# The last addition of eight decoded weight pieces, moved from VectorE to GpSimd

## The chip, the cores and the metric

The kernel runs on one core of a Trainium2 chip. The metric is the device time of one execution, in microseconds, as the median of several runs. The engines are TensorE (PE, with its weight loads as PEld), VectorE (DVE), ScalarE (ACT), GpSimd (POOL) and SyncE (SP), which issues all the transfers here.

## The reference, cut to what matters

Linear attention is followed by a gated feed-forward layer. The feed-forward weights arrive as 64-bit floats.

```python
def phi(x):                                   # per head: 576 x 64 -> 576 x 256
    proj = x @ w_phi
    proj = proj - np.max(np.abs(proj), axis=-1, keepdims=True)
    return np.concatenate([np.exp(proj), np.exp(-proj)], axis=-1)
q_p, k_p = phi(q), phi(k)                     # 8 batches x 8 heads
kv, z = k_p.T @ v, k_p.sum(axis=rows)
attn = (q_p @ kv) / (q_p @ z + 1e-6)
x = attn, heads side by side                  # 4608 x 512
xn = x / sqrt(mean(x * x) + 1e-6) * rms_g
g, val = xn @ w_gate, xn @ w_val              # 512 x 1536 each
out = (silu(g) * val) @ w_out                 # 1536 x 512
```

## The kernel before, in words

**Attention.** The 64 heads are worked off as 32 pairs. A loop of 35 rounds (L524) runs as a pipeline over the pairs. In round i, `front(i)` transposes and projects K and Q of pair i. On PE that is L305 and L318 to L320, on ACT the casts of L60, on DVE the maximum L322 and the subtraction L325 that give `yk` and `yq`. `mid(i-1)` takes the exponentials of pair i-1 and accumulates K^T V: ACT makes `eq` and `qh` (L388, L389), and GpSimd subtracts them into `ql`, eight pieces of 128x256 (L393) and one small one (L395) for each pair. `back(i-2)` multiplies Q's features with K^T V (PE L427) and reads `qh` and `ql`; its K^T V operands are `kv0h`, `kv0l` and `kv1h`, `kv1l` by turns from pair to pair. `last(i-3)` divides (DVE L463, L464) and stores rows of `xs`.

**Decoding.** A 64-bit weight is turned into a 32-bit one in `_decode`, one piece of 128x384 at a time. There are 32 such pieces. ACT scales the high and the low words (L48, L49), DVE does three bit operations (L50 to L52), GpSimd multiplies in two halves of 128x192 (L54), and an addition (L55) finishes the piece. Pieces 0 to 7, four of `w_gate` and four of `w_val`, are the weights of the *fill*: `fill_w` scales each by the norm's weight and splits it on ACT (L241) and DVE (L242) into `fg` or `fv`. The other 24 are only stored to DRAM (L247). The rounds take 0.8 piece each at first and 1.1 from round 10 on (L534).

**Fill.** From round 9 on, blocks of finished attention rows are multiplied with `fg` and `fv` (PE L495) between the attention's own products.

**Order.** The Python loops merge the steps of a round by position (`_merge`, L64). The order in which each engine gets its instructions is not that of the source: the whole program goes through the framework's scheduler (`schedule_with_timeline_sim=True`, L1471), which puts them in order by a timeline of its own when the kernel is built. `late()` (L176) adds one edge: what is traced inside it is issued behind the last instruction that ACT, DVE and GpSimd each had at that place. A decoded piece lies inside it. Behind the attention a second planner (`Flow`) writes out the order by hand, each engine's instruction chained to the one before (line 575 in the profile).

The line of the change passes the adding engine to `_decode` as `add_eng`; before, the condition there is never true for the 32 pieces of this kernel, so all additions are DVE's.

Of the kernel before, what the change touches and what calls it, by code (L numbers as in the profile page):

```python
# [30 lines left out]
def _fetch(nc, pool, src, n):  # L31
    if src.dtype == F32:
        w = pool.tile([128, n], F32, name="wa", bufs=2)
        nc.sync.dma_start(out=w, in_=src)
        return w
    raw = pool.tile([128, n, 2], I32, name="raw", bufs=2)
    nc.sync.dma_start(out=raw.rearrange("p n t -> p (n t)"), in_=src.bitcast(I32))
    return raw


def _decode(nc, pool, raw, n, add_eng=None):
    if raw.dtype == F32:
        return raw
    low, high = raw[:, :, 0], raw[:, :, 1]
    p = pool.tile([128, n], I32, name="wp", bufs=2)
    a = pool.tile([128, n], F32, name="wa", bufs=2)
    u, lf = a.bitcast(I32), low.bitcast(F32)
    nc.scalar.mul(a, high.bitcast(F32), REBASE)  # L48
    nc.scalar.mul(lf, low.bitcast(U32), 2.0 ** -52)  # L49
    nc.vector.tensor_scalar(p, u, 3, None, ALU.logical_shift_left)  # L50
    nc.vector.scalar_tensor_tensor(p, u, -0x80000000, p, ALU.bitwise_and, ALU.bitwise_or)
    nc.vector.tensor_scalar(u, p, -0x00800000, None, ALU.bitwise_and)  # L52
    for h in (slice(0, n // 2), slice(n // 2, n)):
        nc.gpsimd.tensor_tensor(a[:, h], lf[:, h], a[:, h], ALU.mult)  # L54
    (add_eng or nc.vector).tensor_tensor(a, p.bitcast(F32), a, ALU.add)  # L55
    return a
# [26 lines left out]
def kernel(ctx: ExitStack, tc: tile.TileContext, q, k, v, w_phi,  # L83
                         w_gate, w_val, w_out, rms_g, out):
    nc = tc.nc
# [3 lines left out]
    NC, NJ = DM // 128, DF // 128  # L89
# [85 lines left out]
    @contextmanager  # L175
    def late():  # L176

        ins = nc.cur_bb.bb.instructions
        n = len(ins)
        with ExitStack() as es:  # L180
            for eng in LATE:
                for i in reversed(ins[-300:]):
                    if i.engine == eng and i.name not in waiting:
                        es.enter_context(tc.issue_after(i))
                        break
            yield
        waiting.update(i.name for i in nc.cur_bb.bb.instructions[n:])
# [9 lines left out]
    dec = a_ctx.enter_context(tc.tile_pool(name="a_dec", bufs=1))  # L197
# [61 lines left out]
    def decode_pieces(jobs, dec):  # L259
        raws = {}  # L260

        def piece(i):
            if i == 0:
                raws[0] = _fetch(nc, dec, *jobs[0][:2])
            raw = raws.pop(i)
            if i + 1 < len(jobs):
                raws[i + 1] = _fetch(nc, dec, *jobs[i + 1][:2])
            with late():
                jobs[i][2](_decode(nc, dec, raw, jobs[i][1], nc.gpsimd if i >= 2 * NC + 24 else nc.vector))
        return [lambda i=i: piece(i) for i in range(len(jobs))]  # L270

    st = {}
# [397 lines left out]
    nc = Engines()  # L670
# [627 lines left out]
    nc = tc.nc  # L1298
# [177 lines left out]
```

## Time and profile before

| what | value |
|---|---|
| median of 3 runs | 1224.36 us (1223.18 to 1227.45) |
| the profiled execution | 1228.98 us |
| its span on the core | 1227.2 us |
| TensorE busy | 1207.3 us (98%) |
| VectorE, ScalarE, GpSimd busy | 1012.9, 810.3, 620.2 us |
| mean granted TensorE clock | 0.997 |

The span runs from the first to the last instruction of the profiled execution. A share of busy time is a mean over all stages, so the stretches have to be read one by one. Times in the trace count from the start of the span.

### The profile page before, as it was taken

The numbers are of one execution on the slowest core, as the hardware profiler recorded it, in microseconds if no ns is written. First come the engines' busy times: TensorE is split into PE (matmuls) and PEld (weight loads), VectorE is DVE, ScalarE is ACT, GpSimd is POOL, SyncE is SP. The second block draws the span as 40 slices with busy tenths as digits, with TensorE's granted clock in tenths as the row PEclk, the third lists the DMA queues.
The fourth block names the chain that finished last, engine by engine and source line by source line (L and its number), as shares of the span: only waits on it lengthen the run. The fifth ranks groups of instructions, "written<-read, shape, count | busy, mean of one in ns | idle before, by whom it ended". The sixth has DMA issues, their size and how long they took to land.

```text
span 1227.2 us, 28324 instructions
## 1 busy us (share of the span) xinstructions
PE 1207.3 (98%) x10347; PEld 1198.7 (98%) x10347; DVE 1012.9 (83%) x1581; ACT 810.3 (66%) x1867; POOL 620.2 (51%) x681
## 2 busy tenths in 40 slices
PE   8999999999999999999999999999999999999998
PEld 7898999999999999999999999999999999999998
DVE  6889988778788887897996888799777799888884
ACT  6788887778778787667666667667656454444441
POOL 3656664556556666774876777677676200000000
PEclk9999999999999999999999999999999999999999
DMA  5446575657565653986465667755545645544421
GB/s 154 129 122 167 144 207 169 184 158 194 153 176 150 174 160 100 291 267 201 127 206 182 208 198 223 235 175 192 173 154 171 242 142 177 163 139 138 138 95 44
DMA packets 204123, 209.29 MB, mean 171 GB/s; under 512 B 70928, under 2 KB 174224, under 8 KB 201808
## 3 DMA queue, kind: packets, MB, share of 16 engines
q1 hardware_dynamic: 203984, 207.48, 56.1%
q8 instruction: 82, 1.34, 0.5%
q14 instruction: 57, 0.47, 0.1%
HBM read 136.87 MB, written 70.40 MB: 169 GB/s over the span
## 4 chain that ended last, share of the span: by engine, by line
PE 86%; DVE 5%; DMA 4%; ACT 2%; issue 1%; POOL 1%; SPq 0%; DVEq 0%; ACTq 0%; POOLq 0%
PE B L575 12%; PE E L575 10%; PE A L575 9%; PE acc L361 8%; PE gz L1398 6%; PE gy L1398 6%; PE gd L1398 6%; PE fp L495 6%; PE sm L427 5%; PE fp L1398 3%; PE pp L318 3%; PE fp L427 3%; PE pp L320 3%; PE pp L319 2%; PE sm L377 2%; PE sm L305 2%
## 5 line engine op out<-in xcount | busy, mean ns | idle before, releaser
L393 POOL TENSOR_TENSOR ql<-eq,qh 128x256 fp32r<-128x256 f32 x256 | 218.9, 885 | 90.5 <-issue 47.1
L575 PE MATMUL B<-xo,w 128*128 128x256 f32 x1458 | 193.6, 277 | 1.8 <-ACT h L575 1.2
L575 PEld LDWEIGHTS B<-xo,w 128*128 128x128 f32 x1458 | 178.4, 188 | 3.2 <-ACT h L575 2.0
L322 DVE TENSOR_REDUCE mx<-pp 128x4 f32<-128x512 f32 (+1 forms) x160 | 101.2, 634 | 53.8 <-PE pp L320 52.1
L575 PE MATMUL A<-xo,w 128*128 128x256 f32 x972 | 137.1, 277 | 0.0
L575 PE MATMUL E<-xo,w 128*128 128x256 f32 x972 | 137.1, 277 | 0.0
L361 PE MATMUL acc<-vm,ek 128*128 128x65 f32 x1024 | 130.4, 269 | 0.0
L361 PEld LDWEIGHTS acc<-vm,ek 128*128 128x128 f32 x1024 | 126.6, 193 | 0.0
L575 PEld LDWEIGHTS E<-xo,w 128*128 128x128 f32 x972 | 122.9, 188 | 0.2
L575 PEld LDWEIGHTS A<-xo,w 128*128 128x128 f32 x972 | 122.8, 188 | 0.3
L575 POOL TENSOR_TENSOR h<-h,c 128x256 f32<-128x256 f32 x81 | 65.8, 812 | 88.9 <-ACT h L575 77.7
L389 ACT ACTIVATE qh<-sm 128x512 fp32r<-128x512 f32 (+1 forms) x192 | 97.1, 506 | 0.0
L60 ACT CAST xo<-st 128x768 fp32r<-128x768 f32 x54 | 44.9, 838 | 70.5 <-PE gy L1398 25.6
L388 ACT ACTIVATE eq<-sm 128x512 f32<-128x512 f32 x128 | 78.3, 612 | 15.2 <-PE sm L377 14.8
L318 PE MATMUL pp<-wh,th 128*128 128x256 f32 x288 | 86.5, 302 | 1.8 <-DVE yk L325 0.7
L320 PE MATMUL pp<-wh,tl 128*128 128x256 f32 x288 | 83.3, 298 | 0.0
L319 PE MATMUL pp<-wl,th 128*128 128x256 f32 x288 | 81.5, 284 | 0.0
L575 ACT ACTIVATE h<-A 128x256 f32<-128x256 f32 x81 | 31.2, 385 | 73.9 <-PE A L575 56.2
L1398 PE MATMUL gy<-w,xo 128*128 128x256 f32 x648 | 78.4, 279 | 0.2 <-ACT xo L60 0.2
L348 ACT ACTIVATE ek<-yk 128x512 f32<-128x512 f32 x128 | 75.4, 647 | 2.8 <-DVE yk L325 2.8
L1398 PE MATMUL gd<-w,xo 128*128 128x256 f32 x648 | 76.7, 276 | 0.0
L1398 PE MATMUL gz<-w,xo 128*128 128x256 f32 x648 | 76.7, 276 | 0.0
(195 smaller groups left out, 3370.3 us busy)
## 6 DMA issues: line engine op xcount, KB each, us to landing
w<-hs SPq DMA_DIRECT2D x17, 1536.0 KB
hs<-h SPq DMA_DIRECT2D x81, 256.0 KB
gvs<-fo SPq DMA_DIRECT2D x108, 128.0 KB
gvr<-gvs SPq DMA_DIRECT2D x54, 256.0 KB
x<-xs SPq DMA_DIRECT2D x18, 512.0 KB
x<-xs SPq DMA_DIRECT2D x9, 1024.0 KB
rc<-di SPq DMA_DIRECT2D x31, 288.0 KB
kt<-in_k_dram SPq DMA_DIRECT2D x32, 256.0 KB
```

The source lines that it names most:

```text
L318: nc.tensor.matmul(o, th[:, cs], wh, start=True, stop=False)
L319: nc.tensor.matmul(o, th[:, cs], wl, start=False, stop=False)
L320: nc.tensor.matmul(o, tl[:, cs], wh, start=False, stop=True)
L322: nc.vector.tensor_reduce(mx[:, 0:2 * m], pp[:, 0:2 * m], axis=AX.X, op=ALU.max, apply_absolute_value=True)
L348: nc.scalar.activation(e[h][:, sg], y["k", h], AF.Exp, scale=1.0 - 2.0 * sg)
L361: nc.tensor.matmul(acc[:, sg, h], e[h][:, sg, j], vm[:, h, j], start=False, stop=(h == 1 and j == T0 - 1))
L388: nc.scalar.activation(ei[:, sg], yi, AF.Exp, scale=1.0 - 2.0 * sg)
L389: nc.scalar.activation(hi[:, sg], yi, AF.Exp, scale=1.0 - 2.0 * sg)
L393: nc.gpsimd.tensor_tensor(lo[:, sg, cs], ei[:, sg, cs], hi[:, sg, cs].bitcast(F32), ALU.subtract)
L427: nc.tensor.matmul(o[:, 0:m], a[:, h, sg], e[:, sg, h, cs], start=(i == 0), stop=(i == 5))
L575: r = f(*a, **k)
L1398: nc.tensor.matmul(place[n], a[:, kp], w[:, o], start=(first and (kp, i) == turns[0]), stop=((kp, i) == turns[-1]), skip_group_check=True)
```

## The change

For pieces 0 to 7 the addition L55 is issued by GpSimd, right behind its two products L54 in the source. Nothing else differs: the same operands, the same tiles, the same `late()` block. Pieces 8 to 31 keep VectorE.

```diff
             with late():
-                jobs[i][2](_decode(nc, dec, raw, jobs[i][1], nc.gpsimd if i >= 2 * NC + 24 else nc.vector))
+                jobs[i][2](_decode(nc, dec, raw, jobs[i][1], nc.gpsimd if i >= 2 * NC + 24 or i < 2 * NC else nc.vector))
```

`NC` is 4. The addition itself is the last line of `_decode`:

```python
(add_eng or nc.vector).tensor_tensor(a, p.bitcast(F32), a, ALU.add)
```

## Rows read from the trace of the kernel before

**Rows 1.** The page, part 1: busy time and share of each engine.

```profile
PE 1207.3 (98%) x10347; PEld 1198.7 (98%) x10347; DVE 1012.9 (83%) x1581; ACT 810.3 (66%) x1867; POOL 620.2 (51%) x681
```

**Rows 2.** Windows: busy time (instructions) of each engine, then clock, DMA share, GB/s.

```profile
50.44:59.97 9.53, 7.91 (x46) 6.91 (x45) 6.53 (x13) 6.87 (x16) 8.04 (x10) 0.82 0.43 124
...
110.00:120.00 10.00, 10.00 (x84) 9.78 (x83) 9.87 (x17) 8.16 (x23) 4.78 (x5) 1.00 0.63 180
...
160.00:475.00 315.00, 314.50 (x2688) 313.54 (x2687) 256.47 (x454) 254.01 (x636) 182.18 (x228) 1.00 0.61 168
```

**Rows 3.** Waits of PE, 0 to 150 us: total us, times, longest.

```profile
PE sm L377 <- DVE yq L325: 2.6, 4, 1.3
...
PE fp L427 <- ACT kv1h L60: 0.7, 1, 0.7
PE pp L318 <- DVE yk L325: 0.7, 2, 0.5
PE fp L427 <- ACT kv0h L60: 0.6, 2, 0.4
PE fp L427 <- DVE kv0l L61: 0.6, 1, 0.6
```

**Rows 4.** Line 55, 0 to 150 us: duration ns min/median/max, first and last start.

```profile
L55 DVE TENSOR_TENSOR wa<-wp,wa x8: 546/850/1074, 30.3 to 139.4; 128x384 f32<-128x384 f32 x8
```

**Rows 5.** GpSimd's two-input operations of two widths, with min/median/max ns.

```profile
L393 POOL TENSOR_TENSOR ql<-eq,qh x84: 717/740/1295, 19.5 to 156.9; 128x256 fp32r<-128x256 f32 x84
...
L575 POOL TENSOR_TENSOR ri<-ri,t x27: 1283/1477/1770, 506.2 to 854.0; 128x512 f32<-128x512 f32 x27
```

**Rows 6.** Timeline of ACT, DVE, POOL: first, sixth and last of the pieces.

```profile
29.08 1.16 POOL L54 TENSOR_TENSOR wa<-raw,wa 128x192 f32<-128x192 f32 x2 [2.51 <-ACT th L60]
31.64 0.67 ACT L241 ACTIVATE fg<-wa,g 128x384 fp32r<-128x384 f32 x1
...
109.08 1.69 POOL L54 TENSOR_TENSOR wa<-raw,wa 128x192 f32<-128x192 f32 x2
...
111.39 4.01 POOL L393 TENSOR_TENSOR ql<-eq,qh 128x256 fp32r<-128x256 f32 x4 [0.62 <-POOL wa L54]
...
113.92 0.88 DVE L55 TENSOR_TENSOR wa<-wp,wa 128x384 f32<-128x384 f32 x1
...
114.83 0.62 ACT L241 ACTIVATE fv<-wa,g 128x384 fp32r<-128x384 f32 x1 [1.84 <-DVE wa L55]
...
136.84 1.17 POOL L54 TENSOR_TENSOR wa<-raw,wa 128x192 f32<-128x192 f32 x2 [0.41 <-POOL ql L393]
139.41 0.55 DVE L55 TENSOR_TENSOR wa<-wp,wa 128x384 f32<-128x384 f32 x1
...
140.47 0.63 ACT L241 ACTIVATE fv<-wa,g 128x384 fp32r<-128x384 f32 x1
```

**Rows 7.** Timeline of PE: the order of L319 and L318, and one wait.

```profile
31.69 0.28 PE L319 MATMUL pp<-wl,th 128*128 128x256 f32 x1
31.80 0.28 PE L318 MATMUL pp<-wh,th 128*128 128x256 f32 x1
...
107.78 0.63 PE L377 MATMUL sm<-ident,yq 128*128 128x128 f32 x4 [1.25 <-DVE yq L325]
```

**Rows 8.** Timeline of DVE ahead of that wait.

```profile
106.22 0.81 DVE L51 SCALAR_TENSOR_TENSOR wp<-wa,wp 128x384 int32<-128x384 int32 x1
106.95 0.68 DVE L325 TENSOR_TENSOR yq<-pp,mx 128x512 f32<-128x512 f32 x1
...
108.15 0.37 DVE L52 TENSOR_SCALAR wa<-wp 128x384 int32<-128x384 int32 x1
```

**Rows 9.** Timeline of GpSimd's `ql` of one pair, and PE's first reading of them.

```profile
52.61 5.86 POOL L393 TENSOR_TENSOR ql<-eq,qh 128x256 fp32r<-128x256 f32 x6
...
67.81 0.31 PE L427 MATMUL fp<-ql,kv1h 128*128 128x320 f32 x1
```

**Rows 10.** Timeline of PE: its first fill products with `fv`.

```profile
145.05 1.63 PE L495 MATMUL fp<-xo,fv 128*128 128x256 f32 x12
```

## The prediction, made before the result was known

> **What bounds the kernel now.** I read the page first, then windows, then TensorE's waits, then the decoded pieces one by one.
>
> TensorE is busy for 1207.3 of the span's 1227.2 us, GpSimd for half of it [rows 1]. That is a mean, so the windows come next. All eight pieces lie between 25 and 145 us. From 160 to 475 us TensorE stands for only 0.5 us in 315 [rows 2]: there neither VectorE nor GpSimd can shorten anything. What can be won or lost lies before 160 us.
>
> The waits say what ends TensorE's gaps there. Apart from the start-up the larger of them make 5.2 us, of which VectorE ends 2.6 + 0.7 + 0.6 = 3.9 us (`yq`, `yk`, `kv0l`) and ScalarE the rest; GpSimd ends none of them [rows 3]. There is one more loss: the granted clock of 50.44 to 59.97 us is 0.82 of full, so about (1 - 0.82) x 9.53 = 1.7 us of it went to the lower level, 1.2 GHz, after a run of short gaps in TensorE's work [rows 2]. The most that any relief could give back is thus 5.2 + 1.7 = 6.9 us, and a few tenths of smaller gaps.
>
> **What the change removes.** Eight additions leave VectorE: 546 to 1074 ns each, median 850, one by one 1.07 + 0.55 + 0.56 + 0.99 + 0.85 + 0.88 + 0.85 + 0.55 = 6.30 us [rows 4]; the sixth and the last of them stand in [rows 6]. The question is whether TensorE was waiting for what stood behind them. I looked behind each of the eight: no gap of TensorE begins within 2 us after one that its successors on VectorE could have ended. The largest of VectorE's gaps, 1.25 us at 107.78, shows what it is instead [rows 7]: `yq` at 106.95 runs right behind the bit operation L51, 0.81 us at 106.22 [rows 8], and that stays. Where VectorE is fullest, 9.87 of 10 us, TensorE is busy for all 10 [rows 2]. So I cost the removal at nothing. The cover is TensorE's backlog of work already released; if it were gone, a median addition would be worth 0.85 us, and all eight 6.3 us at most.
>
> **What it adds.** No row shows GpSimd adding 128x384. GpSimd's two-input operations take 717 to 1295 ns at 256 columns (median 740) and 1283 to 1770 ns at 512 (median 1477) [rows 5]. Half way between the smallest is 1.00 us, between the largest 1.53, between the medians 1.11. I take 1.05, nearer the low end because the median at 256 columns lies close to its minimum: 8 x 1.05 = 8.4 us more on GpSimd, bounds 8.0 and 12.3.
>
> What queues behind it is `ql`. The eight wide `ql` pieces of the pair around 52 us are done at 52.61 + 5.86 = 58.47, and TensorE reads the first of them at 67.81 [rows 9]: 9.3 us of slack, against 1.05 of delay. That is the busiest round for GpSimd that I found. ScalarE reuses the two `eq` buffers that `ql` reads; its waits name GpSimd nowhere in this stretch. So the added work costs nothing too; without that slack it would be 8.4 us.
>
> **What it moves.** The addition's reader is ScalarE's L241. Today the chain goes from GpSimd's products to VectorE's queue to ScalarE; with the change VectorE drops out. The distance from the end of L54 to the start of L241 is, piece by piece, 1.40, 2.23, 3.12, 3.59, 3.87, 4.06, 2.42, 2.46 us, in sum 23.15; the first, the sixth and the last can be read in [rows 6]. An addition of 1.05 us directly behind its products fits into every one of them. In the sixth the products end at 110.77 and VectorE comes to the addition only at 113.92, and ScalarE stands 1.84 us for it [rows 6]; that wait would go. It is worth nothing, since TensorE is busy for all of 110 to 120 [rows 2]. The fill is no nearer to its limit: the last piece's L241 starts at 140.47 [rows 6], TensorE's first product with `fv` at 145.05 [rows 10]. No transfer is issued differently.
>
> **The scheduler.** The order on the engines isn't the source's: TensorE runs L319 and then the next L318 before the L320 that stands between them in the source [rows 7]. The scheduler works with its own price for the moved operation, so the order of other instructions in the attention may change as well. No row prices this. The gain is bounded by the 6.9 us of gaps and clock; for the loss I take as much again, since a new order would have to double all of today's gaps. Near zero is the value I take: three quarters of the attention run at a full TensorE [rows 2], where another order has nothing to move.
>
> The undisturbed addition on VectorE takes 0.546 us [rows 4], on GpSimd 1.05 by my estimate, a ratio of 1.9; against the median of 0.85 it is 1.2. The Trainium skill, GPSIMD Engine Reference, section "When to use GPSIMD", speaks against the change: two-input elementwise work belongs on VectorE, GpSimd being about twice as slow. The lower ratio comes from VectorE's own spread: the same instruction takes 0.55 us at 139.41, after GpSimd's last operation has ended at 138.01, and 0.88 at 113.92, in the middle of GpSimd's 4.01 us of `ql` [rows 6]. The same page, section "Specifications", says that an SBUF interface is shared with VectorE instructions of two SBUF inputs, and these two rows agree. By that rule GpSimd's new 8.4 us would slow what VectorE runs beside them, by at most 0.53 us a piece (1.074 less 0.546), 4.2 in all, and VectorE would be relieved by 2.1 us instead of 6.3. That changes nothing in a sum in which the relief is worth zero.
>
> **Sum.** The profiled execution took 1228.98 us, 1.78 more than its span. Removed 0, added 0, moved 0, order 0: 1229.0 for it. It lies 4.6 us above the median of the runs shown, so the forecast is the median, 1224.4 us.
>
> **The rivals.**
>
> *VectorE's relief reaches TensorE.* The gaps that VectorE ends close, 3.9 us, and with them the stretch of lower clock, 1.7 us. 1224.4 - 5.6 = 1218.8. For it: 6.3 us of VectorE's work go, partly where VectorE is busy for 9.87 of 10 us [rows 2], and `yq` and `yk` are its work. Against: no gap lies behind an addition. It decides from 3.7 us on, two thirds of it.
>
> *ScalarE stands at L241 behind GpSimd's queue; this is the slower side.* If the scheduler puts a block of four `ql` between the products and the addition, 4 x 0.74 = 2.96 us [rows 5], the addition ends 2.96 + 1.05 = 4.0 us behind the products. Set against the eight distances above, ScalarE would be late by 2.6, 1.8, 0.9, 0.4, 0.1, 0, 1.6 and 1.6: 9.0 us of standing, with `kv0h`, `th` and the exponentials queued behind it, for which TensorE waits. If half of it reaches TensorE, 1224.4 + 4.5 = 1228.9. For it: dependent steps of a piece on VectorE have other work between them (L51 and L52 in rows 8). Against: with one or two `ql` between, 0.74 each, all but the first piece or two still fit, and the 1.84 us that ScalarE stood before cost TensorE nothing. It decides where more than 3.7 of the 9.0 us arrive.
>
> *The order shifts by luck.* Gaps come and go, with either sign, by up to about 3 us: 1221.4 to 1227.4, which can't be told from no change.
>
> That the change might do nothing is excluded: the eight pieces are in the trace on VectorE [rows 4].
>
> **How the numbers follow.** About 0.3%, 3.7 us, is what a measurement of this kernel can tell from no change. Forecast and luck within it together: 0.70. Relief reaching TensorE: 0.17. ScalarE behind GpSimd: 0.13. Faster 0.17, same 0.70, slower 0.13. The range reaches to both rivals' values, 1218.8 and 1228.9, and leaves out the halves of them that go further: 1219 to 1229. The likeliest case alone is 1221.4 to 1227.4.
>
> **What would show it.** L55 should appear as eight additions on GpSimd of 1.0 to 1.5 us, and 24 on VectorE. VectorE's busy time should fall by 2 to 6 us, GpSimd's rise by 8 to 12. TensorE's waits before 160 us should stay between 3 and 8 us, with no GpSimd among the releasers, and 160 to 475 us should stay full. I would be wrong if TensorE's waits named L241's successors or `ql`, if the stretch of lower clock vanished or came twice, or if the order of the attention changed so far that gaps appear behind 160 us.

## The result, and the profile after

The changed kernel is slower: 1233.65 us (median of 4 runs, 1233.33 to 1234.99) against 1224.24 (4 runs in the same comparison), a ratio of 1.0077 with a 95% interval of 1.0062 to 1.0092. The forecast was 1224.4, its range 1219 to 1229: the time lies above the range, and the sign was given 0.13. Here and below, ratios leave out the few slow executions (mean clock 0.95 or less: one each of e5, e10 and before), while medians in us include them.

The profiled execution of the kernel after took 1233.75 us (span 1232.0). Its engines, by part 1 of the page, against [rows 1]:

```profile
PE 1208.4 (98%) x10347; PEld 1199.2 (97%) x10347; DVE 1012.4 (82%) x1573; ACT 811.6 (66%) x1867; POOL 631.9 (51%) x689
```

The eight additions have changed engine: eight instructions fewer on VectorE, eight more on GpSimd. But VectorE is no less busy (1012.4 us against 1012.9), which is the first surprise. Line 55 of the kernel after, 0 to 150 us, its duration (min/median/max in ns) and who waited for it, against [rows 4]:

```profile
L55 POOL TENSOR_TENSOR wa<-wp,wa x8: 999/1180/1527, 32.1 to 140.6; 128x384 f32<-128x384 f32 x8
...
  ACT fv L241: 1.4, 1
  ACT fg L241: 0.4, 1
```

On GpSimd an addition takes 1.0 to 1.5 us, and ScalarE stood behind it for 1.8 us in all. So the moved work is about as forecast. The loss must be elsewhere. The windows of the kernel after, for the same stretches as [rows 2] (busy time and instructions of PE, PEld, DVE, ACT, POOL, then clock, DMA share, GB/s):

```profile
50.44:59.97 9.53, 7.33 (x44) 6.42 (x43) 8.32 (x13) 8.09 (x18) 8.55 (x11) 0.83 0.47 137
...
110.00:120.00 10.00, 10.00 (x88) 10.00 (x86) 9.72 (x18) 8.29 (x23) 7.99 (x8) 1.00 0.48 132
160.00:475.00 315.00, 313.73 (x2674) 312.05 (x2673) 256.79 (x451) 252.03 (x632) 182.50 (x224) 1.00 0.62 169
```

From 160 to 475 us TensorE now stands for 1.27 us instead of 0.50: something moved even where the attention was full. The waits of TensorE, 0 to 150 us (total us, times, longest), against [rows 3]:

```profile
PE sm L377 <- DVE yq L325: 3.2, 4, 1.4
PE pp L318 <- DVE yk L325: 1.3, 2, 0.7
PE fp L427 <- DVE kv1l L61: 1.2, 1, 1.2
PE fp L427 <- DVE kv0l L61: 1.2, 1, 1.2
PE pp L318 <- ACT th L60: 1.0, 2, 0.5
...
PE fp L427 <- ACT kv0h L60: 0.5, 2, 0.3
```

VectorE ends 6.9 us of waits here, against 3.9 before. The wait for `kv1l` is new, that for `kv0l` has doubled, those for `yq` and `yk` are 0.6 longer each in sum. Start-up aside, none names GpSimd, and the waits have grown from 5.8 to 8.6 us together. Where the new wait comes from can be seen on VectorE, in the timeline of the kernel after (start, duration):

```profile
95.68 0.69 DVE L325 TENSOR_TENSOR yq<-pp,mx 128x512 f32<-128x512 f32 x1
96.29 1.17 DVE L463 TENSOR_TENSOR nd<-nd,rc 64x576 f32<-64x576 f32 x1
97.48 1.19 DVE L464 TENSOR_TENSOR nd<-nd,rc 64x576 f32<-64x576 f32 x1
98.70 0.22 DVE L445 RECIPROCAL dr<-dr 128x9 f32<-128x9 f32 x1
98.83 0.37 DVE L61 TENSOR_TENSOR kv1l<-acc,kv1h 128x260 fp32r<-128x260 f32 x1
```

The low half of K^T V, 0.37 us of work that TensorE needs at once, now stands behind two divisions whose result is only stored. In the kernel before, the same `kv1l` ran at 93.99, ahead of the second `yq` and of the divisions. The scheduler has put it elsewhere, and not only it: in the tables that hold the two orders in e1 and e3 below, 1,417 of TensorE's 2,757 places differ, 269 of ScalarE's 812, 141 of VectorE's 608 and 172 of SyncE's 479. TensorE's two waits for such low halves, in its timeline (in brackets idle time and who ended it):

```profile
57.06 0.64 PE L427 MATMUL fp<-qh,kv0l 128*128 128x320 f32 x1 [1.22 <-DVE kv0l L61]
...
99.25 0.41 PE L427 MATMUL fp<-qh,kv1l 128*128 128x320 f32 x1 [1.22 <-DVE kv1l L61]
```

`kv0l` is another case than `kv1l`: in both kernels it stands behind the two divisions of its round. What has changed is the first division. Before, and below it after:

```profile
52.56 0.74 DVE L463 TENSOR_TENSOR nd<-nd,rc 64x576 f32<-64x576 f32 x1
...
54.67 0.37 DVE L61 TENSOR_TENSOR kv0l<-acc,kv0h 128x260 fp32r<-128x260 f32 x1
...
55.09 0.41 PE L427 MATMUL fp<-qh,kv0l 128*128 128x320 f32 x1 [0.56 <-DVE kv0l L61]
```

```profile
53.93 1.34 DVE L463 TENSOR_TENSOR nd<-nd,rc 64x576 f32<-64x576 f32 x1
...
56.64 0.37 DVE L61 TENSOR_TENSOR kv0l<-acc,kv0h 128x260 fp32r<-128x260 f32 x1
```

The division takes 0.60 us longer, TensorE's wait grows by 0.66. The moved addition is not what lengthens it: that starts only at 55.83 us, and in e3 below, where the addition is back on VectorE, the division takes 1.34 us too.

Last, the clock. Windows of the kernel after, PE alone (width, busy time, clock, DMA share, GB/s):

```profile
54.00:66.00 12.00, 10.28 (x71) 0.86 0.40 125
96.00:111.00 15.00, 13.28 (x108) 1.00 0.68 183
970.00:980.00 10.00, 8.48 (x58) 0.83 0.78 286
```

Two stretches ran in part at the lower level, 1.2 GHz: 0.14 x 12 = 1.7 us and 0.17 x 10 = 1.7 us were lost to it. The profiled execution of before also has a stretch near 55 us [rows 2] and one near 970, and its mean granted clock is 0.997 as well. At that equal clock the two executions are 1233.75 - 1228.98 = 4.8 us apart, and TensorE's idle time has grown by 2.6 us before 160 us (10.8 to 13.4) and by 0.8 from 160 to 475. The other 4.7 of the 9.5 us come from what is usual: before's other executions, in all comparisons, mostly had a mean clock of 0.999 to 1.0, after's four had 0.995 to 0.997. So by this one pair about half of the loss is there at an equal clock, and the other half is clock. The split is rough: after's execution at 0.997 took as long (1233.75) as its three at 0.995 (1233.33 to 1234.99). Whether the second follows from the first is for the experiments.

### The profile page after: what moved, and what is told of

Same layout as the page of the kernel before. It is cut to its first block, busy times and chain, and to the rows that moved or that the text cites. A ratio compares the mean times of both kernels' runs of the same rounds, so it can differ in the third digit from the quotient of the medians.

```text
span 1232.0 us, 28322 instructions
## 1 busy us (share of the span) xinstructions
PE 1208.4 (98%) x10347; PEld 1199.2 (97%) x10347; DVE 1012.4 (82%) x1573; ACT 811.6 (66%) x1867; POOL 631.9 (51%) x689
## 3 DMA queue, kind: packets, MB, share of 16 engines
q8 instruction: 82, 1.34, 0.5%
## 4 chain that ended last, share of the span: by engine, by line
PE 89%; DVE 5%; DMA 3%; ACT 1%; issue 1%; SPq 0%; POOL 0%; DVEq 0%; ACTq 0%; POOLq 0%
PE B L575 12%; PE A L575 10%; PE E L575 9%; PE acc L361 8%; PE fp L495 6%; PE gz L1398 6%; PE gy L1398 6%; PE gd L1398 6%; PE sm L427 5%; PE fp L427 3%; PE fp L1398 3%; PE pp L318 3%; PE pp L320 3%; PE pp L319 2%; PE sm L377 2%; PE sm L305 2%
## 5 line engine op out<-in xcount | busy, mean ns | idle before, releaser
L318 PE MATMUL pp<-wh,th 128*128 128x256 f32 x288 | 87.0, 304 | 2.7 <-DVE yk L325 1.3
L319 PE MATMUL pp<-wl,th 128*128 128x256 f32 x288 | 81.8, 286 | 0.0
```

What stands on the lines that cost most here:

```text
L318: nc.tensor.matmul(o, th[:, cs], wh, start=True, stop=False)
L319: nc.tensor.matmul(o, th[:, cs], wl, start=False, stop=False)
```

## The experiments

**Theories.** One: the addition's new engine costs, through its duration, its queue or its contention with VectorE. Two: the new order costs, either everywhere or in a few places. In most of the runs below the order on each engine is held by edges added in the source after tracing, one instruction behind the other; a table says which order.

**e1, the control.** The kernel before with its own order held.

```diff
+    for e, order in ORDER:                    # one list of instructions for each engine
+        last = None
+        for n in order:
+            i = traced[n]
+            if last is not None:
+                tc.add_manual_dep(i, last.name, NoSync, reason="order")
+            last = i
```

> Control: the kernel before, unchanged in its work, with the order that the scheduler had given it written out as a chain of issue-order edges for each engine over the whole attention. Both theories expect the time of before, 1224 us, within 2 us. If it differs by more, holding an order costs something itself, and the next two kernels are to be read against this one.

Measured: 1224.91 us, ratio 1.0002 (0.9994 to 1.0011). Holding an order costs nothing that can be measured.

**e2, the additions on GpSimd in before's order.** The change, with each addition right behind its products on GpSimd and everything else where before has it.

```diff
-    add_eng = nc.gpsimd if i >= 2 * NC + 24 else nc.vector
+    add_eng = nc.gpsimd if i >= 2 * NC + 24 or i < 2 * NC else nc.vector
+    ORDER = before's, the eight additions behind their products on GpSimd
```

> The eight additions on GpSimd, directly behind their two products, everything else on every engine in the order of the kernel before. Theory A (the new order of the other instructions costs the time, the moved work nothing): 1224 us, within 2 us of the control. Theory B (the moved work costs it: ScalarE's cast stands behind GpSimd, or the ql queue behind the addition): 1232 to 1235 us, as the changed kernel. Between 1227 and 1231: both have a share.

Measured: 1224.58 us, 1.0004 (0.9993 to 1.0015). Line 55 and VectorE around 94 us in this run:

```profile
L55 POOL TENSOR_TENSOR wa<-wp,wa x8: 1001/1208/1450, 31.3 to 136.8; 128x384 f32<-128x384 f32 x8
```

```profile
93.56 0.43 DVE L61 TENSOR_TENSOR kv1l<-acc,kv1h 128x260 fp32r<-128x260 f32 x1
93.90 0.68 DVE L325 TENSOR_TENSOR yq<-pp,mx 128x512 f32<-128x512 f32 x1
94.50 1.10 DVE L463 TENSOR_TENSOR nd<-nd,rc 64x576 f32<-64x576 f32 x1
```

The additions are as long as in the kernel after, nobody waits for them, and no time that can be measured is lost. The first theory falls with this run.

**e3, the additions on VectorE in after's order.** The reverse: the order without the change.

```diff
     add_eng = nc.gpsimd if i >= 2 * NC + 24 else nc.vector
+    ORDER = after's, the eight additions back at before's places on VectorE
```

> The eight additions back on VectorE, each behind the same VectorE instruction as in the kernel before, all other instructions of every engine in the order that the scheduler gave the changed kernel. Theory A: 1232 to 1235 us, as the changed kernel, though no work has moved. Theory B: 1224 us, as before, within 2 us.

Measured: 1235.73 us, 1.0095 (1.008 to 1.0109). Waits and windows of PE:

```profile
PE fp L427 <- DVE kv1l L61: 2.1, 1, 2.1
PE fp L427 <- DVE kv0l L61: 1.2, 1, 1.2
```

```profile
54.00:66.00 12.00, 10.28 (x72) 0.86 0.41 122
96.00:111.00 15.00, 12.41 (x73) 0.77 0.59 171
```

The order alone, with no addition on GpSimd, costs as much or more. With the additions back on VectorE, `kv1l` is later still, and a second stretch of lower clock follows it.

**e4, the first four pieces alone, scheduler free.**

```diff
-    nc.gpsimd if i >= 2 * NC + 24 or i < 2 * NC else nc.vector
+    nc.gpsimd if i >= 2 * NC + 24 or i < NC else nc.vector
```

> Only pieces 0 to 3 (those of w_gate) are added on GpSimd; the scheduler is free, as in the changed kernel. Theory B, cost per moved addition: half of the 9.4 us, so about 1229 us. Theory A: what the order happens to be, anywhere between 1221 and 1236 us; a time outside 1227 to 1231 speaks for A.

Measured: 1229.28 us, 1.0041 (1.0028 to 1.0053), with the same two waits of 1.2 us for low halves. The order tips with the early pieces: `kv1l` at 97 us is late although the piece beside it is not moved.

**e5, the first piece's place.** In before's order (with the additions on GpSimd) the first piece is put where after has it. There `yk` comes out late behind it.

```diff
  VectorE:  L322 mx
-           L242 fg        (first piece)
            L322 mx
+           L242 fg
  ScalarE:  L241 fg behind one more nd (L435);  GpSimd:  L55 behind two ql (L393)
```

> The order of e2 (additions on GpSimd, all else as before), except for the first piece: as in the changed kernel, two ql pieces stand between the products and the addition on GpSimd, L241 stands behind one nd copy on ScalarE, and L242 stands behind two mx on VectorE. Three engines, eight instructions. Theory A1 (the cost sits in few places on VectorE's queue): TensorE's waits for yk, yq and kv0l before 58 us grow by 2 us, and a stretch of 3.4 us at the lower clock comes back at 54 us and costs 1.7: 1227 to 1229 us. Theory A2 (the cost is spread over the hundreds of other shuffled instructions): 1224 to 1225.5 us.

Measured: 1229.49 us, 1.0032 (1.0016 to 1.0048). It costs about 3.9 us by itself, by the ratio. No waits are read from its profile.

**e6, one low half.** In the order of e2 a single instruction is moved.

```diff
  VectorE:  L325 yq
-           L61  kv1l      (94 us)
            L325 yq
            L463 nd
            L464 nd
            L445 dr
+           L61  kv1l
```

> The order of e2 with one instruction moved: VectorE's kv1l of the round around 94 us stands behind yq, the two divisions L463 and L464 and the reciprocal L445, as in the changed kernel. Theory A1: TensorE waits 1.2 us for it, with 0.5 for th beside it and at times a stretch at the lower clock (1.7 us each): 1225.5 to 1228 us. Theory A2: 1224 to 1225 us.

Measured: 1234.04 us, 1.0075 (1.0053 to 1.0098). One instruction of 0.4 us in another place costs as much as the whole change, three times the wait that it causes. TensorE's timeline and windows show how:

```profile
97.86 0.63 PE L427 MATMUL fp<-qh,kv1l 128*128 128x320 f32 x1 [2.99 <-DVE kv1l L61]
```

```profile
94.00:96.00 2.00, 0.87 (x7) 1.00 0.63 158
97.00:99.00 2.00, 1.14 (x4) 0.50 0.45 163
...
107.00:109.00 2.00, 2.00 (x11) 0.50 0.80 218
109.00:111.00 2.00, 2.00 (x14) 0.76 1.00 308
111.00:113.00 2.00, 2.00 (x22) 1.00 1.12 330
```

The reader is to see the clock column. TensorE stands for 2.99 us, and when it starts again it runs at 0.50 until 109 us and is back at full by 111, though it is busy for every microsecond between. It does 11 products in 2 us there, 22 afterwards. From its restart at 97.86 to 111 us the clock has a mean of 0.54: 0.46 x 13.1 = 6.0 us lost to the clock, plus 3.0 of wait, is 9.0; measured were 9.4 (1234.04 less 1224.59, the median of before in the same comparison). The stretch near 55 us, which e6's profile has as before's has it, is not in this sum. That this equals the loss of the kernel after is chance: there the wait for `kv1l` is 1.22 us, and the clock is full from 96 to 111 us.

**e7, two places of after mended.** After's order with the first piece and `kv1l` as e2 has them.

```diff
  after's order:
+ VectorE L242 fg, ScalarE L241 fg, GpSimd L55 of the first piece: back to e2's places
+ VectorE L61 kv1l (97 us): ahead of yq and the divisions
```

> The order of the changed kernel, hundreds of shuffled instructions on TensorE, ScalarE and SyncE included, with the two places mended: the first piece's addition, L241 and L242 stand where e2 has them, and kv1l stands ahead of the divisions. Theory A1: most of the 9.4 us comes back, 1225 to 1228 us. Theory A2: 1231 to 1234 us.

Measured: 1230.41 us, 1.004 (1.0024 to 1.0056). A part comes back, less than expected; the wait of 1.2 us for `kv0l` is still there. Its twelve executions fall into two groups: four with a mean clock of 0.998 or 0.999 took 1226.5 to 1227.4 us, seven with 0.996 or 0.997 took 1228.7 to 1233.1. The twelfth, the profiled one, took 1232.48 at a mean clock of 1.0: from 16 to 27 us TensorE did 61 products in it and 99 in the kernel after, busy throughout in both. The mean clock does not show every loss.

**e8, more places moved forward.** In e2's order, six VectorE instructions are put further ahead than before has them.

```diff
  VectorE:  +kv0l (55 us) ahead of the divisions
            +yq ahead of the bit operations L51, L52 in three rounds
```

> The order of e2 with six VectorE instructions moved the other way, at the places of TensorE's longest waits in the kernel before: yq ahead of the bit operations L51 or L52 in three rounds, and kv0l at 55 us ahead of the divisions. Theory A1: the waits for yq (1.25, 0.4 and 0.4 us) and for kv0l (0.6 to 0.8) shrink by 2 us together, 1221.5 to 1223 us, faster than both kernels. Theory A2: 1224 to 1225 us.

Measured: 1223.85 us, 0.9998 (0.9983 to 1.0013): no gain that can be measured, though `yq` falls to 1.6 us of waits.

**e9, a quarter of the delay.** As e6, but `kv1l` stands behind the second `yq` only.

```diff
  VectorE:  L325 yq
-           L61  kv1l
            L325 yq
+           L61  kv1l
            L463 nd
```

> The order of the run with the adds on GpSimd in before's order, and one VectorE instruction moved: the low half of kv at 94 us stands behind the next query subtraction (yq) alone, not behind the two divisions and the wide add too. That is a quarter of the delay which cost 9.5 us. If a gap is only as long as itself (the prediction's way of counting), the wait for it on TensorE grows by 0.3 to 0.6 us and the time is 1224.5 to 1225.5. If the cost is a step that comes with a lower clock once the gap is long enough, then either nothing is seen (no stretch of half clock near 95 us, 1224 to 1225.5) or the stretch is there at its full length (about 13 us, 1231 to 1235). A time between, near 1227, would speak for a cost that grows with the gap's length.

Measured: 1227.12 us, 1.002 (1.0008 to 1.0031), a time between. The wait for `kv1l` in the profiled execution is 0.3 us, and the clock stays full behind it:

```profile
54.00:66.00 12.00, 11.17 (x80) 0.86 0.35 103
96.00:111.00 15.00, 13.56 (x113) 1.00 0.69 184
970.00:980.00 10.00, 10.00 (x77) 0.83 0.48 177
```

Its twelve executions spread: five at a mean clock of 0.999 or 1.0 took 1224.6 to 1226.5, seven at 0.996 to 0.998 took 1226.1 to 1229.9. So most of the loss here goes with how often an execution gets stretches of the lower clock. That the moved instruction brings them is not shown: in the profiled execution they lie at other places, one of them ahead of it.

**e10, the third place of after mended too.** As e7, with `kv0l` at 55 us ahead of the divisions.

```diff
  VectorE, after's order as in e7:
            L325 yq
+           L61  kv0l      (55 us)
            L463 nd
            L464 nd
            L445 dr
-           L61  kv0l
```

> After's order with the two places of the run before last mended (the first piece's block, the low half of kv at 94 us) and a third: the low half of kv at 55 us is put ahead of the two divisions and the wide add behind which it stands. If the lost time lies in the few places where VectorE's order makes TensorE wait, the wait for kv0l (1.2 us) goes and the time falls from 1230.4 to 1225 to 1229. If what is left belongs to the order of TensorE's own instructions (about 1,400 places differ from before), nothing changes: 1229.5 to 1231.5.

Measured: 1225.36 us, 1.0006 (0.9997 to 1.0016). With five instructions moved (`kv1l` and three of the first piece put back, `kv0l` put ahead of where either kernel has it) the loss is gone, although the orders on TensorE, ScalarE and SyncE are still after's but for two places: 1,417, 267 and 172 places differ from before.

**e11 and e12, a rule in the source, scheduler free.** The divisions of a round are issued behind that round's low half; once in the kernel after (e11) and once in before (e12).

```diff
             _split(nc, kh[:, :, :, 0:D + 1], kl[:, :, :, 0:D + 1], av)
+            low = the last VectorE instruction traced
+            while held:                       # the two divisions of this round
+                tc.add_manual_dep(held.pop(), low.name, NoSync, reason="kv first")
```

> The kernel after, its order left to the scheduler again, with one rule added in the source: VectorE issues the two divisions of a round behind that round's low half of kv. The table of an order is not used. If late low halves of kv cause the loss, the waits for kv0l and kv1l go, the stretches of half clock behind them too, and the time is 1226 to 1229 (the misplaced first piece stays). If the loss comes from a new order as such, whichever it is, the rule gives yet another order and 1231 to 1234.

> The kernel before with the same rule in the source (the adds stay on VectorE, the scheduler is free). Before has one wait for a low half of kv, of 0.7 us, and almost none of the half clock. If late low halves are what costs, it gains at most that: 1222 to 1224.5. If any new order loses by chance, 1225 to 1233.

Measured: e11 1229.84 us, 1.004 (1.0024 to 1.0055); e12 1223.53, 0.9993 (0.9983 to 1.0003). In e11 the waits for low halves shrink to 0.3 us each, but the scheduler makes yet another order, and that has waits of its own:

```profile
108.13 0.63 PE L381 MATMUL sm<-ident,yq 128*128 128x128 f32 x4 [1.67 <-DVE yq L326]
109.98 0.38 PE L319 MATMUL pp<-wh,th 128*128 128x256 f32 x1 [1.23 <-ACT th L60]
```

Before gains nothing that can be measured from the rule.

**e13 and e14, how the loss divides.** After's order with only the two low halves mended (e13), or only the first piece (e14).

```diff
  e13:  + VectorE kv0l (55 us) and kv1l (97 us) ahead of the divisions
  e14:  + the first piece's L242, L241 and L55 back to e2's places
```

> After's order with the two low halves of kv (at 55 and at 97 us) put ahead of the divisions, and nothing else: the first piece's block stays as it is in after. If the first piece's place costs TensorE something of its own (alone in before's order it cost 3.9 us, TensorE waiting 0.5 us longer for yk), the time is 1227 to 1230. If the two low halves are the whole cause, 1224.5 to 1226.5.

> After's order with the first piece's block mended, and nothing else: both low halves of kv stay behind the divisions. If the low halves are the main cause, most of the loss stays: 1230 to 1234. If the first piece sets the phase of all that follows, 1225 to 1228.

Measured: e13 1225.85 us, 1.0012 (1.0003 to 1.002); e14 1230.64, 1.0049 (1.0033 to 1.0064). Two instructions on VectorE give back 7.8 of the 9.4 us. The windows of e13 against those of the kernel after, above:

```profile
54.00:66.00 12.00, 11.50 (x97) 1.00 0.44 123
96.00:111.00 15.00, 15.00 (x131) 1.00 0.70 198
970.00:980.00 10.00, 10.00 (x91) 1.00 0.58 212
```

The clock is full in all three. From 96 to 111 us TensorE does not stand at all, but only because all is 3 us earlier: the waits for `yq` (0.56) and `th` (0.50) ahead of `kv1l` end at 92.25 and 94.56 us here, at 95.20 and 97.53 in the kernel after. In sum they are what they were, and only those for the low halves are gone:

```profile
PE sm L377 <- DVE yq L325: 3.2, 4, 1.4
PE pp L318 <- ACT th L60: 1.0, 2, 0.5
```

The lower clock has become rarer with them: the mean clock of e13's twelve executions is 0.998 to 1.0. In e14 the two waits of 1.2 us remain, and a longer stretch of lower clock follows the first:

```profile
PE fp L427 <- DVE kv0l L61: 1.2, 1, 1.2
PE fp L427 <- DVE kv1l L61: 1.2, 1, 1.2
```

```profile
54.00:66.00 12.00, 10.27 (x56) 0.72 0.40 112
```

The two mends do not add up (7.8 and 3.0 us, where both together, in e10, give back 8.3). That each changes how long the clock is low would explain it, but is not shown.

Of the two low halves `kv0l` seems to weigh more. From e14 to e7 only `kv1l` is mended, and nothing measurable comes back (1230.64 to 1230.41); from e7 to e10 only `kv0l` is moved, and 5.0 us do (1230.41 to 1225.36). In before's order, where `kv0l` stands behind the same divisions and TensorE waits 0.6 to 0.8 us for it, the runs that move it ahead, among other things, gain nothing that can be measured (e8, e12). No run mends `kv0l` alone in after's order.

**e15, the late low half with the additions on VectorE.** e6's move in the kernel before.

```diff
  VectorE, before's order:
-           L61  kv1l      ahead of yq, L463, L464, L445
+           L61  kv1l      behind them
```

> Before's order with the additions on VectorE, and the one low half of kv at 94 us behind the divisions. With the additions on GpSimd the same move cost 9.5 us and one wait of 3.0 us; there the first of the two divisions took 1.33 us, where it took 0.74 in before. If the addition on GpSimd lengthens the division, the wait is 2.3 to 2.5 us here and the time 1229 to 1233; if where the addition runs has no part in it, the wait is 2.9 to 3.1 us and the time 1232 to 1235.

Measured: 1232.62 us, 1.0058 (1.0039 to 1.0077). VectorE, and below it TensorE:

```profile
94.57 0.94 DVE L463 TENSOR_TENSOR nd<-nd,rc 64x576 f32<-64x576 f32 x1
```

```profile
97.29 0.63 PE L427 MATMUL fp<-qh,kv1l 128*128 128x320 f32 x1 [2.60 <-DVE kv1l L61]
```

The division takes 0.94 us here and 1.33 in e6, and the wait is 2.60 instead of 2.99. So 0.4 us of that wait go with the addition on GpSimd; the rest, and the lower clock behind it (0.54 over 96 to 111 us here as well), belong to the order. The two times can't be told apart. Five of the six executions had a mean clock of 0.994 and took 1232.0 to 1234.4 us; the sixth had 1.0 and took 1227.64, which is 3.3 us above before (1224.35) and near the length of the wait. By this one execution the late instruction costs little more than its wait where the clock stays full; where it fell, the loss was 7.6 to 10.0 us.

## Why the prediction failed

**The step that failed** is the scheduler's new order: "Near zero is the value I take", and "for the loss I take as much again, since a new order would have to double all of today's gaps". It measured 9.4 us, more than the 6.9 allowed. Most of it, 7.8 us, came with the waits for two instructions of 0.4 us each (e13), 1.22 us a wait, and no doubling of all gaps was needed. One of the two, `kv1l`, had been moved; the other, `kv0l`, kept its place on VectorE and came late because the division ahead of it took 1.34 instead of 0.74 us. And the step priced gaps mainly by their length. In e6 a wait of 2.99 us cost 9.4, because the clock fell to 1.2 GHz and stayed there through 12 us of uninterrupted work. The prediction had the row for such a cost, the 0.82 of 50.44 to 59.97 us [rows 2], but let the 1.7 us lost there double at most.

A second part of the step was too narrow: "three quarters of the attention run at a full TensorE [rows 2], where another order has nothing to move". They did stay nearly full (0.8 us more of standing from 160 to 475 us), but the early quarter was enough.

**What held.** The relief of VectorE at nothing: e2 has it without the new order, and the time is 1.0004. GpSimd's addition at 1.05 us: it took 1.00 to 1.53, median 1.18, within the bounds, GpSimd's busy time rose by 11.7 us, and the slack was there. The moved chain at nothing: ScalarE stood behind the addition for 1.8 us in the kernel after, in e2 not at all, and neither shows up in TensorE's waits.

**The rivals.** That VectorE's relief reaches TensorE is refuted by e2. ScalarE behind GpSimd's queue was the slower side, at 1228.9: its mechanism did occur (GpSimd has two `ql` between products and addition in the first piece), but with 1.8 us of standing instead of 9.0 and without TensorE waiting for it. The first piece costs in another way: L242 moves behind a second maximum, and TensorE's wait for the `yk` behind it is 0.7 us, as e13 has it too; in e2 TensorE stands at that place for 0.2, and not for VectorE. The true rival was the third, shifts by luck, whose price of about 3 us was too small by a factor of three.

**VectorE's busy time** was to fall by 2 to 6 us and fell by 0.5. The eight additions, 6.3 us, did go, but the sixteen divisions L463 and L464 before 160 us grew from 14.0 to 17.9 us in sum (means 799 and 956 ns before, 1095 and 1136 after). With the order held, from e1 to e2, they grew from 14.0 to 16.7. The Trainium skill, GPSIMD Engine Reference, section "Specifications", says that the SBUF interface is shared with VectorE instructions of two SBUF inputs; these divisions are such instructions, and the sums of e1 and e2 agree. They don't say which division is slowed: in before the one of 0.74 us at 52.56 has `ql` beside it as well. In e2 the time shows no cost of it (1.0004), though TensorE's wait for `kv0l` is 0.8 us there instead of 0.6. The same page's section "When to use GPSIMD" has two-input work at about half of VectorE's speed; the medians here are 1180 against 850 ns, 1.4, and the smallest are 999 against 546, 1.8.

**The profiled execution.** The prediction set 4.6 us between the profiled execution of before and the median aside. 3.4 of them were two stretches of lower clock, near 55 and near 970 us (0.86 over 12 us and 0.83 over 10), which most executions of that kernel do not have, by their mean clocks of 0.999 to 1.0.

**What stays open.** Why the scheduler's timeline puts `kv1l` behind the divisions once additions move to GpSimd: e4 shows that the first four pieces are enough, and no run looked into its prices. Which of the other changed places makes the division ahead of `kv0l` longer, and how after's 9.4 us divide between the two low halves, is open too. The remaining 1.5 us of e13 fit the first piece (`yk`, 0.7 us of wait), but e5's 3.9 us in another order show that such sums don't carry over. Why e9's executions had stretches of lower clock more often than e2's is not shown either.

## What to carry to other kernels

Where a scheduler orders the program at build time, moving an instruction is two changes: the work and the order. Measure the first with the order held before judging it, and then look in the order for short instructions that TensorE reads at once and that stand behind long ones that nobody waits for: two of them were worth 7.8 us here, one of which had stood behind such operations before at no measurable cost. Price a new TensorE gap by the clock that may follow it, not by its length.

## What the runs showed of the hardware

- Behind one wait of 2.99 us TensorE ran at half clock for 12 us without a pause (e6). Behind waits of 0.26, 0.50 and 1.22 us within 4 us it ran at half clock for about 3.4 us (the kernel after, 0.14 x 12 = 1.7 us lost), in e14 for twice that (0.28 x 12 = 3.4), and in e7's profile, with waits of 0.25, 0.50 and 1.22 us, not at all (1.00 from 54 to 66 us). The cost of a late instruction was thus anything from little more than the length of its wait (one execution of e15, 3.3 for 2.60) to three times that (e6, 9.4 for 2.99).
- The same order does not always get the same clock: up to 94 us e6 and e2 issue the same on VectorE, and 54 to 66 us ran at 0.86 in the one's profile and at 1.00 in the other's.
- The first division (64x576) of the round at 94 us took 0.74 us on VectorE in before and 0.94 in e15, where GpSimd's addition is not beside it, and 1.10 (e2) and 1.33 (e6), where it is; but also 1.17 in the kernel after, beside `ql` alone.
